# Attention backward: where the transposed output is scaled, and the order of matmuls around it

## The chip, the core and the metric

The kernel runs on one core of a Trainium2 chip. The core has five engines that run their own instruction queues, in order, and wait for each other through semaphores: TensorE (PE in the profile; its weight loads are PEld), VectorE (DVE), ScalarE (ACT), GpSimd (POOL) and SyncE (SP, which here issues DMAs). The metric is the device time of one execution in microseconds; lower is better.

## The reference

Forward and backward of two attention blocks on 2048 tokens, 16 heads of 28 channels: block A is linear attention, block B is softmax attention with one k and one v shared by all heads (MQA). The outputs are the forward result and the gradients of all eight inputs. The change lies in block B:

```python
def _B_ref(x, wq, wk, wv, wo):
    q = (x @ wq).reshape(B, S, H, Dh).transpose(0, 2, 1, 3)
    k = x @ wk
    v = x @ wv
    scores = jnp.einsum("bhqd,bkd->bhqk", q, k) * (Dh ** -0.5)
    p = _softmax(scores, axis=-1)
    o = jnp.einsum("bhqk,bkd->bhqd", p, v)
    return o.transpose(0, 2, 1, 3).reshape(B, S, H * Dh) @ wo
...
_out, _vjp = jax.vjp(_f, A_x, A_wqkv, A_wo, B_x, B_wq, B_wk, B_wv, B_wo)
_grads = _vjp(grad_out)
```

With e = exp(scores) unnormalised, l its row sums, and do the gradient that reaches o, the backward needs o/l, do/l, the row sum D of do times o/l, then dP = (do/l) v, dS = e (dP - D/l), and from these dQ, dK and dV.

## The kernel before

Block A and the projections of block B come first (up to about 205 us of the profile), then one long loop for the attention of block B, then the last projections. The change is in the loop alone. Its order of instructions is written by hand: the program text is the order of each engine's queue.

**Blocks and units.** A block b (64 of them) is 256 queries by two heads; eight units cover its 2048 keys, 256 keys to a unit (two tiles of 128). The loop runs over units u. At unit u it makes scores and exp of unit u, and, 16 units behind, dP and dS of unit w = u - 16. "Unit n" below is a unit with u mod 8 = n; `due(u, lag)` names the block whose first unit was `lag` units ago, so `due(u, 10)` holds in every unit 2.

**One unit, by engine.**
- TensorE: `rows_SD` issues eight matmuls of 32 rows by 128, 256 columns each. In its list `todo`, (0, h) is the scores of head h, (1, h) is dP of head h; each stands twice, for the two key tiles ("first half" and "second half"). The four kinds use four different groups of 32 rows of the array. Scores go to two of three PSUM banks `SB` in turn, dP to the two banks `DB`.
- ScalarE: exp of head 0 (L946), a copy of head 1's dP to SBUF (L960), exp of head 1 (L992).
- VectorE: dS of head 0 = dP times e, out of PSUM (L958), then a block transpose of the dS of unit u - 18 (L1039).
- GpSimd: dS of head 1 from ScalarE's copy (L961). It can't read PSUM.
- Even units: `o_dq` on TensorE, the "end product", accumulates o and dQ for two units in the bank `oq`. Odd units: `dk_m` accumulates dK (sixteen 32x32 matmuls of 512 columns).
- Every fourth unit SP issues a DMA transpose of eT to eN (L994), which dV reads: `dv_mm`, four matmuls a group, four groups a block, in even units behind `o_dq`.

**Once a block** o must be transposed, scaled and used. Unit 1: VectorE copies o from `oq` to `oTs` (L974). Unit 2: TensorE transposes it (`onat_T`, L809) into the `spare` bank, which is the bank of the scores just consumed and becomes the bank of head 0's scores of the next unit; then `o_norm`: VectorE takes 1/l from it (L818) and multiplies o by it into SBUF (L819); GpSimd makes the product do times o (L823), scales do (L826) and puts o over do in `do_nat` (L827, a cast). Unit 3: VectorE writes dQ of an older block (L977). Unit 4: `row_D`: VectorE sums the products along rows (L831), GpSimd multiplies by 1/l (L832). Unit 6: `don_T` transposes the scaled do (L840) into the spare bank, VectorE copies it out (L847). Unit 0, in most blocks: the output projection into the spare bank (`out_proj`), copied out by VectorE (L747). In half of the blocks GpSimd also copies queries twice (L851).

The order in one unit is: `rows_SD`; transposes and projections into the spare bank; exp, L958, L960, L961; `row_D`; L974, L977; `o_norm`; copies; exp of head 1 and the DMA transpose; `dk_m` or `o_dq` and `dv_mm`; L1039.

Of the kernel before, what the change touches and what calls it, by code (L numbers as in the profile page):

```python
# [9 lines left out]
ALU = mybir.AluOpType  # L10
AX = mybir.AxisListType
BF16 = mybir.dt.bfloat16
F32 = mybir.dt.float32
# [4 lines left out]
P = 128  # L18
# [7 lines left out]
def kernel(  # L26
# [21 lines left out]
    nc = tc.nc  # L48
# [39 lines left out]
    def flat(t):  # L88
        return t.rearrange("p a b -> p (a b)")
# [557 lines left out]
    NB = 64  # L647
    NU = NB * 8
    qT_B = [R1[:, g, :] for g in range(4)]
    vaug, kn, do_nat = vaug_, kn_, R2x[:, 0:NS, :]  # L650
    with ExitStack() as cs_:
# [7 lines left out]
        pw_ = cs_.enter_context(tc.tile_pool(name="cwk", bufs=4, side="right"))  # L659
# [5 lines left out]
        dsT, dsx, qX, don, doT, rl, prod = ({} for _ in range(7))  # L665
# [6 lines left out]
        def eN(b, c):  # L672
            return ENs[(2 * b + c // 2) % 6][:, 16 * (c % 2):16 * (c % 2) + 16, :]

        def mmt(out, lhsT, rhs, pos, start, stop):
            nc.tensor.matmul(out, lhsT=lhsT, rhs=rhs, start=start, stop=stop, tile_position=pos,  # L676
                             skip_group_check=True)

        def blk(b):
            qc, pair = divmod(b, 8)  # L680
            return qc, pair, pair // 2, pair % 2

        def rows_SD(u, sp, dp):
            b, tp = divmod(u, 8)
            w = u - 16
            qc, pair, g, hp = blk(b)
            todo = [(0, 0), (0, 1), (1, 0), (1, 1)] * 2
            if sp is not None and dp is not None and u % 2 == 0:
                todo = [(0, 0), (0, 1), (1, 0)] * 2 + [(1, 1)] * 2
            seen = {}  # L690
            for d in todo:
                if (dp if d[0] else sp) is None:
                    continue
                k, h = d
                t2 = seen.get(d, 0)
                seen[d] = 1
                t = 2 * tp + t2
                tc_ = slice(t * P, (t + 1) * P)
                oc = slice(t2 * 256, (t2 + 1) * 256)
                r = 64 * (1 - hp if k else hp) + 32 * h  # L700
                if k:
                    mmt(dp[h][:, oc], vT_rep[r:r + 32, tc_], doT[w // 8][r:r + 32, :], (r, 0), True, True)
                else:
                    mmt(sp[h][:, oc], kT_rep[r:r + 32, tc_], qT_B[g][r:r + 32, qc * 256:(qc + 1) * 256],
                        (r, 0), True, True)
# [8 lines left out]
        oTq = flat(R4).rearrange("p (t k) -> p t k", k=P)  # L714
# [85 lines left out]
        onps, tps2 = {}, {}  # L800

        def due(u, lag):
            b, r = divmod(u - lag, 8)
            return b if r == 0 and 0 <= b < NB else None

        def onat_T(b, bank):
            onp = bank[:, 0:P].rearrange("p (q h c) -> p q h c", q=2, h=2)
            for qb in range(2):
                nc.tensor.transpose(onp[:, qb, :, :].rearrange("p h c -> p (h c)"), oTs[0:64, qb * P:(qb + 1) * P],  # L809
                                    identF[0:64, 0:64], tile_position=(0, 0))  # L810
            onps[b] = onp

        def o_norm(b):
            onp = onps.pop(b)
            qc, pair, g, hp = blk(b)
            r_ = pw_.tile([P, 2, 2, 1], F32, name="rl")
            os_ = oTs[:, 0:P].rearrange("p (q h c) -> p q h c", q=2, h=2)
            nc.vector.reciprocal(out=r_[:], in_=onp[:, :, :, 0:1])  # L818
            nc.vector.tensor_tensor(out=os_, in0=onp[:, :, :, :], in1=r_[:].to_broadcast([P, 2, 2, 32]), op=ALU.mult)  # L819
            rl[b] = r_  # L820
            dnv = do_nat[:, 2 * qc:2 * qc + 2, pair * 64:pair * 64 + 64].rearrange("p q (h c) -> p q h c", c=32)
            prod[b] = pw_.tile([P, 2, 2, 32], F32, name="prod", bufs=1)
            nc.gpsimd.tensor_tensor(out=prod[b][:], in0=dnv, in1=os_, op=ALU.mult)  # L823
            dn = pw_.tile([P, 2, 2, 32], BF16, name="don", bufs=3)
            don[b] = dn
            nc.gpsimd.tensor_tensor(out=dn[:], in0=dnv, in1=r_[:].to_broadcast([P, 2, 2, 32]), op=ALU.mult)  # L826
            nc.gpsimd.tensor_copy(out=dnv, in_=os_)  # L827

        def row_D(b):
            Dq = pw_.tile([P, 2, 2, 1], F32, name="Dq")  # L830
            nc.vector.tensor_reduce(out=Dq[:, :, :, 0], in_=prod[b][:], axis=AX.X, op=ALU.add)  # L831
            nc.gpsimd.tensor_tensor(out=don[b][:, :, :, 0:1], in0=Dq[:], in1=rl[b][:], op=ALU.mult)  # L832

        def don_T(b, bank):
# [14 lines left out]
        def qc_copy(eng, st, qc, g, s):  # L849
            src = qT_B[g][:, qc * 256:(qc + 1) * 256].rearrange("p (b j s) -> p b j s", b=4, s=2)[:, :, :, s]  # L850
            eng.tensor_copy(out=st.rearrange("p (b s) a j -> p b s a j", s=2)[:, :, s, :, :],  # L851
                            in_=src.unsqueeze(2).to_broadcast([P, 4, 4, 32]))
# [36 lines left out]
        def o_dq(vs, ys):  # L889
            for v, y in zip(vs, ys):  # L890
                todo = [f(i) for f, i in ((o_mm, v), (dq_mm, y)) if 0 <= i < NU]
                for _ in range(2):
                    for g_ in todo:
                        next(g_)

        def dv_mm(dv_acc, b, h, qb):
            for c in range(4):
                rhs = eN(b, c).rearrange("p (u h t q) k -> p u h t q k", u=2, h=2,
                                                       t=2)[:, :, h, :, qb, :]
                mmt(dv_acc[32 * c:32 * c + 32, :], don[b][:, qb, h, :], rhs, (0, 32 * c),  # L900
                    b == 0 and h + qb == 0, b == NB - 1 and h + qb == 2)
# [15 lines left out]
        with tc.manual_schedule():  # L917
# [8 lines left out]
            for u in range(NU + 28):  # L926
# [3 lines left out]
                sp = [SB[(2 * u + h) % 3] for h in range(2)] if hasS else None  # L930
                dp = DB if hasD else None
                spare = SB[(2 * u + 2) % 3] if hasS else DB[u // 4 % 2] if u > 530 else SB[2]
                rows_SD(u, sp, dp)
                if (b := due(u, 10)) is not None:
                    onat_T(b, spare)
                if (b := due(u, 14)) is not None:
# [10 lines left out]
                if u == 1:  # L947
                    q_shift(pn3, shifts[3], [pd_.tile([P, 2, 512], BF16, name="dsT").rearrange("p a b -> p (a b)").bitcast(F32)
                                             for _ in range(1)])
                    dv_acc = psA.tile([P, 512], F32, name="aacc")  # L950
# [13 lines left out]
                if 0 <= gq < 4 and u < 448:  # L964
                    if gq == 0 and iq == 0:
                        qX[qq] = (pqb_ if qq % 2 else pqa_).tile([P, 4, 2, 512], BF16, name="qX")
                    if iq < 2:
                        qc_copy(nc.gpsimd, qst, qq, gq, iq)
                if (b := due(u, 12)) is not None:
                    row_D(b)  # L970
                if u == 7:
                    nc.vector.memset(oTs[64:128, :], 0.0)
                if (b := due(u, 9)) is not None:
# [1 line left out]
                if (b := due(u, 27)) is not None:  # L975
                    qc, pair, g, hp = blk(b)
                    nc.vector.tensor_scalar(out=qT_B[g][64 * hp:64 * hp + 64, qc * 256:(qc + 1) * 256],  # L977
                                            in0=oq[64:128, 0:256], scalar1=scale, scalar2=None, op0=ALU.mult)
                if (b := due(u, 10)) is not None:
                    o_norm(b)  # L980
                    if b in (15, 31, 47, 55, 63):
                        t0, t1 = 2 * (b // 8) - 2 * (b < 48), 2 * (b // 8) + 2
                        nc.sync.dma_start_transpose(oTq[:, 4 * (t0 % 4):4 * (t0 % 4) + 4 * (t1 - t0), :],
                                                    do_nat[:, t0:t1, :].rearrange("p q c -> p (q c)"))
                if (b := due(u, 14)) is not None:
                    don_copy(b)
                if op:
# [11 lines left out]
                if u % 2:  # L999
                    b, i = divmod(u - 27, 8)  # L1000
                    if 0 <= b < NB:
                        for m in range(2 * i, 2 * i + 4):
                            dk_m(b, m, (1 + (u == 519 and m == 2 * i + 1)) * (m % 2) if 519 <= u < 537 else 0)
                else:
                    o_dq((u - 2, u - 1), (u - 20, u - 19))
                    b, n = divmod(u - 20, 8)
                    for k in {0: (0, 1), 2: (2,), 6: (3,)}.get(n, ()) if 0 <= b < NB else ():
                        dv_mm(dv_acc, b, k // 2, k % 2)
                y = u - 18

                if 512 <= u < 528 and u % 2 == 0:
# [23 lines left out]
                if 0 <= y < NU:  # L1035
                    b, tp = divmod(y, 8)
                    if tp == 0:
                        dsx[b] = px_.tile([P, 8, 2, 2, 256], BF16, name="dsx")
                    nc.vector.transpose(  # L1039
                        out=dsx[b][:, tp, :, :, :].rearrange("p h t c -> p (h t c)").bitcast(F32),  # L1040
                        in_=dsT[y][:, :, :].rearrange("p h c -> p (h c)").bitcast(F32))

        dkvT, wqT, xb = post["dkvT"], post["wqT"], post["xb"]
        dkvn = post["dkvn"].rearrange("p (t c) -> p t c", c=64)
# [11 lines left out]
        for c in range(4):  # L1056
# [3 lines left out]
                                           in1=dk_sum[32 * c:32 * c + 32, :].rearrange("p (t i) -> p t i", i=32),  # L1060
# [91 lines left out]
```

## Time and profile before

| what | value |
|---|---|
| median of 3 runs | 1053.05 us (1052.27 to 1053.55) |
| profiled execution | 1052.68 us, its span 1050.9 us |
| busy: TensorE matmul, weight loads | 1008.4 us (96%), 486.6 us (46%) |
| busy: VectorE, ScalarE, GpSimd | 895.9 us (85%), 871.5 us (83%), 798.2 us (76%) |
| L961 GpSimd, 512 times | 1156 ns each |
| L1039, L958 VectorE, 512 times each | 699 ns, 668 ns each |
| L946, L960, L992 ScalarE, 512 times each | 612 ns, 617 ns, 629 ns each |
| L818, L819 VectorE, 64 times each | 159 ns, 292 ns each |
| L823, L826, L827, L832 GpSimd, 64 times each | 431, 399, 289, 216 ns each |
| L831, L847, L974, L977 VectorE, 64 times each | 276, 280, 405, 427 ns each |
| granted TensorE clock | full speed |

An engine starts its next instruction while the last results of the one before still drain: three ScalarE instructions of some 0.6 us in a unit of 1.5 us take less than their sum. So the mean duration of an instruction is not the time that it keeps the engine; for that the distance between two starts is read, where the second one waited for nothing. The loop's first exp (L946) starts at 207.7 us and the last at 977.0 us, 512 of them. Times of day in the prediction are microseconds from the start of the span.

### The profile page before, as it was taken

What the parts mean: (1) busy time and instruction counts of PE and PEld (TensorE: products, weight loads), DVE (VectorE), ACT (ScalarE), POOL (GpSimd) and SP (SyncE); (2) the same over time, 40 slices, a digit from 0 to 9 for tenths busy, and PEclk for the clock granted to TensorE, in tenths of its full rate; (3) what the DMA queues carried; (4) which work ended last, traced back from release to release, by engine and by line L of the source; (5) the groups of instructions that cost most, each with busy time, mean ns of one, the idle gap of its engine ahead of it and who ended that gap; (6) DMA issues with size and microseconds to landing.
All of it is one profiled execution on the core that took longest, in us unless ns stands there. A gap on an engine that the chain in (4) does not pass through costs nothing.

```text
span 1050.9 us, 40033 instructions
## 1 busy us (share of the span) xinstructions
PE 1008.4 (96%) x16236; PEld 486.6 (46%) x16245; DVE 895.9 (85%) x1781; ACT 871.5 (83%) x1743; POOL 798.2 (76%) x1044
## 2 busy tenths in 40 slices
PE   9999999998999999999999999999999999999998
PEld 5555554434444444444444444444444444444444
DVE  6897500669999999999999999999999999999942
ACT  6463122589999999999999999999999999999632
POOL 8601272238888998899899989988998999888860
PEclk9999999999999999999999999999999999999999
DMA  9879999299999999999999999999999999999973
GB/s 266 150 134 192 189 222 215 42 163 202 188 196 190 188 195 198 194 193 191 197 175 195 192 202 185 204 199 184 192 194 191 194 190 193 204 186 182 220 156 87
DMA packets 689058, 195.15 MB, mean 186 GB/s; under 512 B 670408, under 2 KB 686688, under 8 KB 688872
## 3 DMA queue, kind: packets, MB, share of 16 engines
q1 hardware_dynamic: 680392, 179.97, 102.1%
q0 software_dynamic: 4544, 9.46, 3.4%
q10 hardware_dynamic: 3936, 3.16, 1.0%
q8 instruction: 127, 2.08, 0.8%
q14 instruction: 59, 0.48, 0.1%
HBM read 12.60 MB, written 10.84 MB: 22 GB/s over the span
## 4 chain that ended last, share of the span: by engine, by line
PE 44%; ACT 33%; issue 14%; DVE 6%; POOL 2%; DMA 0%; ACTq 0%; DVEq 0%; POOLq 0%
ACT cp L960 17%; ACT eT L992 13%; PE agen L81 13%; PE aacc L676 10%; PE agen L676 10%; PE aacc L81 6%; ACT eT L946 2%; DVE dsT L958 2%; PE aacc L809 2%; DVE dsx L1039 2%; PE aacc L840 1%; POOL dsT L961 1%; DMA out_dram<-dsT 0%; PE agen L313 0%; PE agen L227 0%
## 5 line engine op out<-in xcount | busy, mean ns | idle before, releaser
L961 POOL TENSOR_TENSOR dsT<-cp,eT 128x512 bf16<-128x512 bf16 x512 | 587.7, 1156 | 78.9 <-ACT cp L960 73.2
L1039 DVE STREAM_TRANSPOSE dsx<-dsT 128x512 f32<-128x512 f32 x512 | 357.8, 699 | 2.8 <-POOL dsT L961 0.7
L676 PEld LDWEIGHTS <-R 32*128 32x128 bf16 (+1 forms) x9104 | 228.5, 94 | 275.0 <-issue 239.4
L958 DVE TENSOR_TENSOR dsT<-agen,eT 128x512 bf16<-128x512 f32 x512 | 341.9, 668 | 10.6 <-PE agen L676 5.4
L960 ACT ACTIVATE cp<-agen 128x512 bf16<-128x512 f32 x512 | 315.8, 617 | 11.5 <-PE agen L676 10.5
L946 ACT ACTIVATE eT<-aacc 128x512 bf16<-128x512 f32 x512 | 313.6, 612 | 13.6 <-PE aacc L676 4.3
L992 ACT ACTIVATE eT<-aacc 128x512 bf16<-128x512 f32 x512 | 322.2, 629 | 0.0
L676 PE MATMUL agen<-dsx,qX 32*32 32x512 bf16 x4024 | 264.0, 376 | 0.0
L676 PE MATMUL agen<-doT,R 32*128 32x256 bf16 x2048 | 246.7, 269 | 4.2 <-DVE dsT L958 2.5
L676 PE MATMUL aacc<-R,R 32*128 32x256 bf16 (+1 forms) x2240 | 218.5, 269 | 7.1 <-DVE oTs L819 2.0
L676 PE MATMUL agen<-eT,R 128*32 128x256 bf16 x2048 | 157.4, 274 | 0.1
L676 PE MATMUL agen<-dsT,R 128*32 128x256 bf16 x2048 | 156.6, 274 | 0.1
L676 PEld LDWEIGHTS <-qX 32*32 32x32 bf16 x4096 | 78.2, 89 | 111.7 <-issue 53.3
L676 PE MATMUL aacc<-eN,don 128*32 128x512 bf16 x1024 | 96.7, 379 | 0.0
L81 PEld LDWEIGHTS <-R 128*128 128x128 bf16 x517 | 40.9, 98 | 42.2 <-issue 12.0
L81 PE MATMUL agen<-R,R 128*128 128x448 bf16 (+1 forms) x174 | 41.1, 360 | 1.8 <-ACT R L229 0.8
L851 POOL COPY qst<-R 128x512 bf16<-128x512 bf16 x56 | 34.2, 611 | 2.9 <-DMA qX<-qst 2.8
L823 POOL TENSOR_TENSOR prod<-R,oTs 128x128 f32<-128x128 bf16 x64 | 27.6, 431 | 9.3 <-DVE oTs L819 9.3
L676 PEld LDWEIGHTS <-don 128*32 128x32 bf16 x1024 | 33.8, 97 | 0.5
L586 DVE TENSOR_TENSOR osb<-R 32x512 bf16<-32x512 bf16 x4 | 1.7, 413 | 34.7 <-ACT R L583 34.7
L262 POOL TENSOR_SCALAR wdq<-wdq 128x448 bf16<-128x448 bf16 x16 | 21.1, 1327 | 12.9 <-DVE phiT L243 12.9
L427 POOL COPY pk<-R 128x256 bf16<-128x256 bf16 x4 | 1.6, 399 | 37.7 <-DVE R L389 37.7
(234 smaller groups left out, 983.1 us busy)
## 6 DMA issues: line engine op xcount, KB each, us to landing
eN<-eT SPq DMA_TRANSPOSE x128
xa<-in_A_x_dram SPq DMA_DIRECT2D x8, 224.0 KB
ga<-in_grad_out_dram SPq DMA_DIRECT2D x4, 448.0 KB
out_dram<-osb ACTq DMA_DIRECT2D x16, 112.0 KB
xa<-in_grad_out_dram POOLq DMA_DIRECT2D x4, 448.0 KB, 9.4
out_dram<-wdq POOLq DMA_DIRECT2D x8, 224.0 KB, 5.8
eT<-in_grad_out_dram SPq DMA_DIRECT2D x4, 448.0 KB
eT<-in_B_x_dram SPq DMA_DIRECT2D x4, 448.0 KB
```

The lines of the kernel that those rows point to most:

```text
L81: nc.tensor.matmul(out_ap, lhsT=lhsT, rhs=rhs, start=start, stop=stop, tile_position=(0, 0))
L262: nc.gpsimd.tensor_scalar(out=wq_n[:, st, 0:D], in0=wq_n[:, st, 0:D], scalar1=1.0, scalar2=None, op0=ALU.min)
L676: nc.tensor.matmul(out, lhsT=lhsT, rhs=rhs, start=start, stop=stop, tile_position=pos, skip_group_check=True)
L809: nc.tensor.transpose(onp[:, qb, :, :].rearrange("p h c -> p (h c)"), oTs[0:64, qb * P:(qb + 1) * P], identF[0:64, 0:64], tile_position=(0 ...
L823: nc.gpsimd.tensor_tensor(out=prod[b][:], in0=dnv, in1=os_, op=ALU.mult)
L851: eng.tensor_copy(out=st.rearrange("p (b s) a j -> p b s a j", s=2)[:, :, s, :, :], in_=src.unsqueeze(2).to_broadcast([P, 4, 4, 32]))
L946: nc.scalar.activation(out=eT(u)[:, 0, :], in_=sp[0][:, :], func=ACT.Exp, scale=scale)
L958: nc.vector.tensor_tensor(out=dst[:, 0, :], in0=dp[0][:, :], in1=ew[:, 0, :], op=ALU.mult)
L960: nc.scalar.activation(out=cp[:, :], in_=dp[1][:, :], func=ACT.Copy)
L961: nc.gpsimd.tensor_tensor(out=dst[:, 1, :], in0=cp[:, :], in1=ew[:, 1, :], op=ALU.mult)
L992: nc.scalar.activation(out=eT(u)[:, 1, :], in_=sp[1][:, :], func=ACT.Exp, scale=scale)
L1039: nc.vector.transpose(out=dsx[b][:, tp, :, :, :].rearrange("p h t c -> p (h t c)").bitcast(F32), in_=dsT[y][:, :, :].rearrange("p h c -> p ...
```

## The change

- In odd units, and in all units at the ends of the loop, `todo` changes: odd units issue all four scores before the four dP; even units keep their list, now also where one of the two streams is absent.
- `o_norm` is split. `o_copy`, at its old place in unit 2, copies the transposed o unscaled out of PSUM to SBUF and has GpSimd make the product do times o. The new `o_norm` stands at the end of the unit, behind L1039: the reciprocal, now from SBUF; GpSimd scales do, and scales o where it cast it before. The DMA transposes of `do_nat` move with it.
- `row_D` moves from unit 4, ahead of L1039, to the end of unit 3, behind L1039. As the product now holds unscaled o, GpSimd multiplies the row sum by 1/l once more.
- `dv_mm` moves from behind `o_dq` to directly behind `rows_SD`, and its fourth group from unit 2 (of the next block) to unit 0.

```diff
-            todo = [(0, 0), (0, 1), (1, 0), (1, 1)] * 2
-            if sp is not None and dp is not None and u % 2 == 0:
+            todo = [(0, 0), (0, 1)] * 2 + [(1, 0), (1, 1)] * 2
+            if u % 2 == 0:
                 todo = [(0, 0), (0, 1), (1, 0)] * 2 + [(1, 1)] * 2
...
-        def o_norm(b):
+        def o_copy(b):
+            qc, pair, g, hp = blk(b)
             onp = onps.pop(b)
-            qc, pair, g, hp = blk(b)
-            r_ = pw_.tile([P, 2, 2, 1], F32, name="rl")
             os_ = oTs[:, 0:P].rearrange("p (q h c) -> p q h c", q=2, h=2)
-            nc.vector.reciprocal(out=r_[:], in_=onp[:, :, :, 0:1])
-            nc.vector.tensor_tensor(out=os_, in0=onp[:, :, :, :], in1=r_[:].to_broadcast([P, 2, 2, 32]), op=ALU.mult)
-            rl[b] = r_
+            nc.vector.tensor_copy(out=os_, in_=onp)
             dnv = do_nat[:, 2 * qc:2 * qc + 2, pair * 64:pair * 64 + 64].rearrange("p q (h c) -> p q h c", c=32)
+            onps[b] = os_, dnv
             prod[b] = pw_.tile([P, 2, 2, 32], F32, name="prod", bufs=1)
             nc.gpsimd.tensor_tensor(out=prod[b][:], in0=dnv, in1=os_, op=ALU.mult)
+
+        def o_norm(b):
+            os_, dnv = onps.pop(b)
+            r_ = pw_.tile([P, 2, 2, 1], F32, name="rl")
+            nc.vector.reciprocal(out=r_[:], in_=os_[:, :, :, 0:1])
+            rl[b] = r_
             dn = pw_.tile([P, 2, 2, 32], BF16, name="don", bufs=3)
             don[b] = dn
             nc.gpsimd.tensor_tensor(out=dn[:], in0=dnv, in1=r_[:].to_broadcast([P, 2, 2, 32]), op=ALU.mult)
-            nc.gpsimd.tensor_copy(out=dnv, in_=os_)
+            nc.gpsimd.tensor_tensor(out=dnv, in0=os_, in1=r_[:].to_broadcast([P, 2, 2, 32]), op=ALU.mult)
 
         def row_D(b):
             Dq = pw_.tile([P, 2, 2, 1], F32, name="Dq")
             nc.vector.tensor_reduce(out=Dq[:, :, :, 0], in_=prod[b][:], axis=AX.X, op=ALU.add)
+            nc.gpsimd.tensor_tensor(out=Dq[:], in0=Dq[:], in1=rl[b][:], op=ALU.mult)
             nc.gpsimd.tensor_tensor(out=don[b][:, :, :, 0:1], in0=Dq[:], in1=rl[b][:], op=ALU.mult)
...
                 rows_SD(u, sp, dp)
+                if u % 2 == 0:
+                    b, n = divmod(u - 20, 8)
+                    for k in {0: (0, 1), 2: (2,), 4: (3,)}.get(n, ()) if 0 <= b < NB else ():
+                        dv_mm(dv_acc, b, k // 2, k % 2)
...
-                if (b := due(u, 12)) is not None:
-                    row_D(b)
...
                 if (b := due(u, 10)) is not None:
-                    o_norm(b)
-                    if b in (15, 31, 47, 55, 63):
-                        t0, t1 = 2 * (b // 8) - 2 * (b < 48), 2 * (b // 8) + 2
-                        nc.sync.dma_start_transpose(oTq[:, 4 * (t0 % 4):4 * (t0 % 4) + 4 * (t1 - t0), :],
-                                                    do_nat[:, t0:t1, :].rearrange("p q c -> p (q c)"))
+                    o_copy(b)
...
                     o_dq((u - 2, u - 1), (u - 20, u - 19))
-                    b, n = divmod(u - 20, 8)
-                    for k in {0: (0, 1), 2: (2,), 6: (3,)}.get(n, ()) if 0 <= b < NB else ():
-                        dv_mm(dv_acc, b, k // 2, k % 2)
...
                         in_=dsT[y][:, :, :].rearrange("p h c -> p (h c)").bitcast(F32))
+                if (b := due(u, 10)) is not None:
+                    o_norm(b)
+                    if b in (15, 31, 47, 55, 63):
+                        t0, t1 = 2 * (b // 8) - 2 * (b < 48), 2 * (b // 8) + 2
+                        nc.sync.dma_start_transpose(oTq[:, 4 * (t0 % 4):4 * (t0 % 4) + 4 * (t1 - t0), :],
+                                                    do_nat[:, t0:t1, :].rearrange("p q c -> p (q c)"))
+                if (b := due(u, 11)) is not None:
+                    row_D(b)
```

## The prediction

> **Names.** A unit is one u of the main loop, a block is eight units, and unit n means u mod 8 = n. A unit has eight 256-column matmuls in `rows_SD`: scores for two heads, each in a first and a second half, and dP likewise. ScalarE takes exp of head 0's scores (L946), copies dP of head 1 (L960), takes exp of head 1's scores (L992). VectorE multiplies dP of head 0 (L958) and transposes (L1039). GpSimd multiplies dP of head 1 (L961).
>
> **What bounds the kernel.** First the busy time of each engine by stretch: the stretch where both streams of the loop run, then one block.
>
> ```profile
> core 0: us, PE busy (x) PEld busy (x) DVE busy (x) ACT busy (x) POOL busy (x), PEclk, DMA share, GB/s
> 250.00:977.00 727.00, 701.29 (x13784) 330.82 (x13783) 710.05 (x1381) 718.98 (x1445) 656.62 (x792) 1.00 1.17 192
> 579.66:591.75 12.09, 11.69 (x231) 5.63 (x231) 11.88 (x24) 12.02 (x26) 11.10 (x14) 1.00 1.19 188
> ```
>
> ScalarE is busy 99% of 727 us, VectorE 98%, GpSimd 90%, at full clock. But these are unions of overlapping instructions, so slack is read from distances between starts. ScalarE in that block:
>
> ```profile
> 580.63 0.66 ACT L992 ACTIVATE eT<-aacc 128x512 bf16<-128x512 f32 x1
> 581.17 0.61 ACT L946 ACTIVATE eT<-aacc 128x512 bf16<-128x512 f32 x1
> ...
> 583.09 0.65 ACT L960 ACTIVATE cp<-agen 128x512 bf16<-128x512 f32 x1
> 583.57 0.66 ACT L992 ACTIVATE eT<-aacc 128x512 bf16<-128x512 f32 x1
> 584.30 0.60 ACT L946 ACTIVATE eT<-aacc 128x512 bf16<-128x512 f32 x1
> ```
>
> Back to back, ScalarE starts one every 0.48 us (583.09 to 583.57). Into an odd unit it starts late: 0.54 into unit 1, 0.73 into unit 3. Read over all blocks between 423.21 and 880.63 us, a block takes 457.4 / 38 = 12.04 us, and L946 of the odd units is late by some 0.06, 0.26, 0.09 and 0.06 us (units 1, 3, 5, 7): 0.47 a block. That is what the change can win from ScalarE, no more.
>
> Unit 3 is late because of VectorE, seen in its timeline in the same block, and TensorE's:
>
> ```profile
> 582.78 0.64 DVE L958 TENSOR_TENSOR dsT<-agen,eT 128x512 bf16<-128x512 f32 x1
> 583.35 0.16 DVE L818 RECIPROCAL rl<-aacc 128x4 f32<-128x4 f32 x1
> 583.54 0.29 DVE L819 TENSOR_TENSOR oTs<-aacc,rl 128x128 f32<-128x128 f32 x1
> 583.75 0.70 DVE L1039 STREAM_TRANSPOSE dsx<-dsT 128x512 f32<-128x512 f32 x1
> 584.38 0.66 DVE L958 TENSOR_TENSOR dsT<-agen,eT 128x512 bf16<-128x512 f32 x1
> ...
> 586.14 0.69 DVE L958 TENSOR_TENSOR dsT<-agen,eT 128x512 bf16<-128x512 f32 x1
> 586.75 0.28 DVE L831 TENSOR_REDUCE Dq<-prod 128x4 f32<-128x128 f32 x1
> 586.94 0.70 DVE L1039 STREAM_TRANSPOSE dsx<-dsT 128x512 f32<-128x512 f32 x1
> ```
> ```profile
> 582.13 0.28 PE L676 MATMUL aacc<-R,R 32*128 32x256 bf16 x2
> ...
> 582.25 0.27 PE L676 MATMUL aacc<-R,R 32*128 32x256 bf16 x2
> ...
> 583.52 0.39 PE L676 MATMUL aacc<-eN,don 128*32 128x512 bf16 x4
> 583.89 0.28 PE L676 MATMUL aacc<-R,R 32*128 32x256 bf16 x2
> ```
>
> The transposed o lies in the bank of the next unit's first scores. It is free when L819 ends (583.84), and the scores start at 583.89, 0.05 later. dV (583.52) fills the time before it. The other odd units are late by order: the second half of the scores stands behind dP of head 1, which waits for L960 of the unit before (580.15 + 0.65 = 580.80; dP issues at 580.85, the scores' second half at 580.86).
>
> **The change, walked through this block.** Distances used: 0.48 between ScalarE's starts (0.49 after it waited); 0.12 from the first to the second half of scores, then 0.27 to its end and 0.03 to L946; 0.05 from the end of a VectorE or ScalarE instruction to the matmul that waits for it; 0.61 to 0.63 from L1039 to L958.
>
> *Scores first.* Unit 1: the second half can issue at 580.81 and end at 581.08; L946 then comes at ScalarE's own pace, 580.63 + 0.48 = 581.11, a gain of 0.06. dP still starts at 580.85, so dK behind it does not move. Where dP waits for nothing, as in unit 3, the odd unit's eight matmuls take longer: dP goes into other rows of the array and issues 0.12 behind the first scores, its second half 0.11 later, so dK starts 0.42 after the first scores, against 0.33 now (583.89 to 584.22).
>
> The Trainium skill says, in "TensorE: Matmul & The Clock Gate", section "The mechanism", that a weight load overlaps running matmuls only in another row group. This order puts two halves of the same rows behind each other, so that rule speaks against it. In this trace the second half at 582.25 starts 0.12 after a first half that runs 0.28, so the load did overlap; the sum goes by that row, and the rule's time is a rival below.
>
> *o copied.* No row shows a 128x128 f32 copy. L819 writes the same shape from the same bank in 292 ns on average, L974 copies 64x256 f32 in 405: I take 0.29 (lower end 0.27, the 112-column cast of L747; upper 0.40). It starts at 583.35 and ends at 583.64, so the scores of unit 3 start at 583.70 instead of 583.89. The four dV matmuls that stood there are gone to unit 0, so TensorE is ready (last product at 583.42 plus about 0.21). With 0.12 + 0.27 + 0.03, L946 comes at 584.11: a gain of 0.19. Without dV's removal it would be held to about 583.88.
>
> *Reciprocal and row sum moved behind L1039.* This gives part back. L1039 starts at 583.55 and ends its turn at 584.16; the reciprocal takes 0.19 (L818's turn today, now from SBUF; 0.12 to 0.30 as bounds), so L958 of unit 3 starts at 584.35 instead of 584.38. Then L977 585.04, L1039 585.39, the reduce 586.00 (its turn 0.19, 0.30 at worst), and L958 of unit 4 at 586.19: 0.05 later than now. Waiting behind it is dP of head 0 in unit 5, which needs L958's end: 586.94 instead of 586.89, and behind that dK and the next scores. GpSimd's product is ready for the reduce: it ends at about 585.3, 0.7 before; were that cover gone, L958 and dK would wait for the whole lack.
>
> *dV ahead.* Per block still sixteen matmuls in four groups, 0.22 a group. In unit 6 a group fills the 0.19 in which the don transposes wait for L992's bank today; in unit 0 one fills the same wait of the output projection (which starts at 579.90 instead of 579.87). In unit 4 two groups only change places with the end product. What they read is old: the transposed eT is issued 13 units (19 us) earlier and the DMA takes 4.8 to 5.9 us. Nothing waits there.
>
> *GpSimd.* The cast of 289 ns (L827) becomes a product (399 to 431 by L826 and L823), and one 128x4 product is added (216 by L832, up to 0.28 with the wait on itself): 0.33 to 0.42 a block. The block shown has the two query copies and 11.10 us busy, so 11.5 of some 11.9. Its dsT are read by L1039 two units later; the latest, now ready at 588.30, would be ready at 588.83, needed at 589.66. Hidden; without that 0.8 it would cost up to 0.4 a block. The five SP transposes of do_nat issue in the same place of SP's queue and wait some 0.1 longer for GpSimd; the next on SP waits for an exp of the next unit anyway. dP-only units at the end get two serial slots more, 0.11 in eight units: 0.4 taken, half of it.
>
> *Sum.* Following on: L946 of unit 5 at 586.98 (now 587.23), of unit 6 at 588.64 (588.67: the late dP has cost TensorE its lead), of unit 7 at 590.09 (590.20), of the next unit 0 at 591.54 (591.65); L958 there 591.64 (591.75). A second block from those times shifts everything by 0.11 again. The block at 604 us, which has no output projection, gives 0.14 by the same steps. With 0.115 a block and 62 blocks: 7.1 us. The profiled execution took 1052.68 (span 1050.9 and 1.8 around it); less 7.1, plus 0.4, is 1046.0, and the median of the runs is 0.37 above that execution: **1046** rounded. Its own range, from gains of 0.03 to 0.25 a block: 1038 to 1051.
>
> **Rivals.**
> - *The waits between engines go too.* VectorE's turns, each at its shortest, sum to about 11.72 a block with output projection; ScalarE's to 24 x 0.48 = 11.5. If only VectorE's turns are left, 0.31 x 62 = 19: 1033. For it: scores no longer wait for dP. Against: VectorE's turns themselves hardly shrink, and dP of unit 5 still hangs on L958.
> - *Nothing comes of it.* VectorE has as many instructions as before and was 98% busy; what leaves unit 2 returns in units 2 and 3: 1053.
> - *VectorE's small jobs hold dP (slower).* Reciprocal and reduce each stand directly before the L958 that frees dP's bank. The row L1039 to L958 is 0.73 into unit 4 today, not 0.62, for a reason that no wait shows. If both jobs carry 0.11 more, L958 of unit 4 comes at about 586.41 and dP of unit 5, dK and L946 of unit 6 are 0.2 later than in the walk, 0.17 later than now; that decides as soon as it exceeds the 0.11 won. A loss of 0.1 a block is 6, with the worst bounds 10: 1059.
> - *The scores' halves run one after another*: if the weights of the second half could load only after the first half has ended, it would start 0.37 (0.28, and 0.09 as the mean of one load) behind the first, L946 of units 1, 3, 7 late by 0.19, 0.07, 0.15, of unit 5 about equal; 0.3 a block after what is won: 1072. The rule of the Trainium skill named above would have it so; the 0.12 at 582.25 speaks against.
>
> **Chances.** Forecast 0.56; waits go too 0.17; nothing 0.12; VectorE's jobs 0.13; halves 0.02. A change of under 0.2% (2.1 us) can't be told from none. So faster 0.73, same 0.12, slower 0.15. The range 1033 to 1058 leaves out half of the second case and half of the slower ones, and holds the bounds of the copy and of the two small jobs.
>
> **What would show it.** The first scores of unit 3 follow the copy by 0.05 and L992-to-L946 there shrinks from 0.73 to about 0.6; in units 1 and 5 it is 0.48 to 0.50; L946 of even units, on pace today, shows some lateness in unit 6; L1039 to L958 into units 3 and 4 is 0.8 with the small job between. I am wrong if L958 of unit 4 is later by more than 0.1, if GpSimd's dsT end VectorE's idle time, or if dK of unit 3 starts more than 0.45 after its scores.

## The result, and the profile after

| | before | after |
|---|---|---|
| median | 1053.14 us (12 runs, 1051.86 to 1054.57) | 1050.93 us (12 runs, 1048.89 to 1052.52) |
| span of the profiled execution | 1050.9 us | 1049.1 us |
| first to last exp of the loop | 769.35 us | 767.93 us |

The ratio is 0.9977 with a 95% interval of 0.9967 to 0.9986: faster by 2.2 us, where 7 were forecast. In the new text exp of head 0 is L955, dS of head 0 L967, the copy of dP L969, dS of head 1 L970, exp of head 1 L995, the copy of o L817, the reciprocal L826, the reduce L835, the dQ write L984, the query copies L856 and their DMA transpose L860, eT's DMA transpose L997.

Busy time by engine over the loop, then ScalarE's timeline in the block from 579 us (start, duration, engine and line):

```profile
core 0: us, PE busy (x) PEld busy (x) DVE busy (x) ACT busy (x) POOL busy (x), PEclk, DMA share, GB/s
250.00:975.00 725.00, 697.21 (x13768) 322.28 (x13762) 705.28 (x1379) 716.17 (x1443) 669.94 (x850) 1.00 1.20 193
```
```profile
583.12 0.69 ACT L995 ACTIVATE eT<-aacc 128x512 bf16<-128x512 f32 x1
583.64 0.66 ACT L955 ACTIVATE eT<-aacc 128x512 bf16<-128x512 f32 x1
...
587.52 0.70 ACT L995 ACTIVATE eT<-aacc 128x512 bf16<-128x512 f32 x1
588.18 0.60 ACT L955 ACTIVATE eT<-aacc 128x512 bf16<-128x512 f32 x1
```

The busy shares hardly tell the two kernels apart, but the distances do. The exp of unit 3 now follows after 0.52 us instead of 0.73. That of unit 6 comes after 0.66: lateness moved three units on. Before, unit 6 kept pace, as here in the kernel before, one block later (0.48):

```profile
600.59 0.60 ACT L992 ACTIVATE eT<-aacc 128x512 bf16<-128x512 f32 x1
601.07 0.62 ACT L946 ACTIVATE eT<-aacc 128x512 bf16<-128x512 f32 x1
```

VectorE and TensorE of the changed kernel, in the stretch from 582 us, show the way it took:

```profile
582.92 0.26 DVE L817 COPY oTs<-aacc 128x128 f32<-128x128 f32 x1
...
583.73 0.12 DVE L826 RECIPROCAL rl<-oTs 128x4 f32<-128x4 f32 x1
583.79 0.65 DVE L967 TENSOR_TENSOR dsT<-agen,eT 128x512 bf16<-128x512 f32 x1
584.47 0.43 DVE L984 TENSOR_SCALAR R<-agen 64x256 bf16<-64x256 f32 x1
...
585.44 0.24 DVE L835 TENSOR_REDUCE Dq<-prod 128x4 f32<-128x128 f32 x1
585.71 0.69 DVE L967 TENSOR_TENSOR dsT<-agen,eT 128x512 bf16<-128x512 f32 x1
```
```profile
583.24 0.28 PE L676 MATMUL aacc<-R,R 32*128 32x256 bf16 x2
...
583.34 0.28 PE L676 MATMUL aacc<-R,R 32*128 32x256 bf16 x2
...
586.13 0.39 PE L676 MATMUL aacc<-R,R 32*128 32x256 bf16 x4
586.46 0.39 PE L676 MATMUL agen<-doT,R 32*128 32x256 bf16 x4
586.78 1.04 PE L676 MATMUL agen<-dsx,qX 32*32 32x512 bf16 x16
587.76 0.28 PE L676 MATMUL aacc<-R,R 32*128 32x256 bf16 x2
```

The copy ends at 583.18 and unit 3's scores start at 583.24. In unit 4 L967 starts 0.27 after the reduce and ends at 586.40; dP of unit 5, whose scores were done issuing by 586.25, starts at 586.46, then dK, and only then the scores of unit 6 (587.76).

So the block is shorter, though by less than forecast. Block lengths are read from the exp of head 0 in every eighth unit. In blocks 16 to 55 plain blocks alternated between 12.03 and 11.97 us before, and take 11.91 or 11.92 now, 0.085 less. In blocks 4 to 14 it is 0.04 less (11.96 now), and in the last seven full ones, from 56 on, 0.02 (12.21 now). Plain blocks alone would so give some 4 us. The rest is lost in four long blocks: blocks 5 and 6 took 13.4 and 13.6 us (13.2 and 12.0 before), blocks 38 and 39 took 12.9 and 12.5 (12.0 and 12.3). All four have query copies or follow a block that has them. The page of the changed kernel names a wait at the query copies (line, count, busy and mean, then idle time before it and its cause), which stood on the page of before with 2.8 us:

```profile
L856 POOL COPY qst<-R 128x512 bf16<-128x512 bf16 x56 | 34.4, 614 | 6.6 <-DMA qX<-qst 5.9
```

One such stall, on SP's, GpSimd's and VectorE's timelines of the changed kernel (idle time and its cause in brackets):

```profile
264.17 11.11 SPq L997 DMA_TRANSPOSE eN<-eT  x2
275.33 1.31 SPq L860 DMA_TRANSPOSE qX<-qst  x1
276.74 10.57 SPq L997 DMA_TRANSPOSE eN<-eT  x2
287.42 2.12 SPq L860 DMA_TRANSPOSE qX<-qst  x1
```
```profile
280.53 0.61 POOL L856 COPY qst<-R 128x512 bf16<-128x512 bf16 x1 [1.94 <-DMA qX<-qst]
```
```profile
282.29 0.71 DVE L1039 STREAM_TRANSPOSE dsx<-dsT 128x512 f32<-128x512 f32 x1 [1.07 <-POOL dsT L970]
```

SP has no gap in which it waits. Two transposes of eT and one of the queries keep it for 12.1 to 12.6 us a block (275.33 to 287.42, and 264.17 to 276.74), more than the block itself takes, so in the four of eight blocks with query copies it can't keep up. In the first such blocks it carries a backlog besides: the exp of unit 27, before any of these copies, ends at 247.35, and its transpose starts at 251.71. The copy at 280.53 may not overwrite the one query buffer before the transpose issued at 275.33 has read it. GpSimd stands for 1.94 us, and VectorE's block transpose waits 1.07 for GpSimd's dS. SP was as full in the kernel before, 12.3 us from one query transpose to the next:

```profile
274.19 1.30 SPq L855 DMA_TRANSPOSE qX<-qst  x1
...
286.45 1.25 SPq L855 DMA_TRANSPOSE qX<-qst  x1
```

### The profile page after: what moved, and what is told of

Read it like the earlier page. It is cut to its first block, busy times and chain, and to the rows that moved or that the text cites. A ratio compares the mean times of both kernels' runs of the same rounds, so it can differ in the third digit from the quotient of the medians.

```text
span 1049.1 us, 40115 instructions
## 1 busy us (share of the span) xinstructions
PE 1006.1 (96%) x16245; PEld 477.9 (46%) x16245; DVE 891.7 (85%) x1781; ACT 870.0 (83%) x1743; POOL 813.8 (78%) x1108
## 3 DMA queue, kind: packets, MB, share of 16 engines
q8 instruction: 127, 2.08, 0.8%
## 4 chain that ended last, share of the span: by engine, by line
PE 61%; DVE 13%; ACT 10%; issue 8%; POOL 7%; DMA 1%; DVEq 0%; POOLq 0%; ACTq 0%
PE agen L676 24%; PE aacc L676 15%; PE agen L81 13%; DVE dsT L967 6%; PE aacc L81 6%; POOL dsT L970 5%; ACT cp L969 4%; ACT eT L995 3%; ACT eT L955 2%; DVE dsx L1039 2%; DVE doT L852 2%; PE aacc L809 2%; DVE Dq L835 1%; DVE R L984 1%; POOL prod L821 1%
## 5 line engine op out<-in xcount | busy, mean ns | idle before, releaser
L970 POOL TENSOR_TENSOR dsT<-cp,eT 128x512 bf16<-128x512 bf16 x512 | 585.6, 1158 | 52.9 <-ACT cp L969 48.4
L1039 DVE STREAM_TRANSPOSE dsx<-dsT 128x512 f32<-128x512 f32 x512 | 357.1, 698 | 5.1 <-POOL dsT L970 3.0
L676 PEld LDWEIGHTS <-R 32*128 32x128 bf16 (+1 forms) x9104 | 239.3, 94 | 258.9 <-issue 209.6
L967 DVE TENSOR_TENSOR dsT<-agen,eT 128x512 bf16<-128x512 f32 x512 | 342.8, 670 | 12.3 <-PE agen L676 5.2
L969 ACT ACTIVATE cp<-agen 128x512 bf16<-128x512 f32 x512 | 324.3, 633 | 13.1 <-PE agen L676 12.7
L955 ACT ACTIVATE eT<-aacc 128x512 bf16<-128x512 f32 x512 | 324.5, 634 | 12.6 <-PE agen L676 4.3
L995 ACT ACTIVATE eT<-aacc 128x512 bf16<-128x512 f32 x512 | 329.7, 644 | 0.0
L676 PE MATMUL agen<-doT,R 32*128 32x256 bf16 x2048 | 242.5, 270 | 7.6 <-DVE dsT L967 4.9
L676 PE MATMUL aacc<-R,R 32*128 32x256 bf16 (+1 forms) x2240 | 208.2, 267 | 19.7 <-DVE doT L852 8.9
L676 PE MATMUL agen<-eT,R 128*32 128x256 bf16 x2048 | 155.3, 273 | 0.1
L676 PE MATMUL aacc<-eN,don 128*32 128x512 bf16 x1024 | 90.5, 387 | 0.0
L856 POOL COPY qst<-R 128x512 bf16<-128x512 bf16 x56 | 34.4, 614 | 6.6 <-DMA qX<-qst 5.9
L676 PEld LDWEIGHTS <-don 128*32 128x32 bf16 x1024 | 20.8, 93 | 40.6 <-issue 40.6
```

The source lines that it names most:

```text
L955: nc.scalar.activation(out=eT(u)[:, 0, :], in_=sp[0][:, :], func=ACT.Exp, scale=scale)
L967: nc.vector.tensor_tensor(out=dst[:, 0, :], in0=dp[0][:, :], in1=ew[:, 0, :], op=ALU.mult)
L969: nc.scalar.activation(out=cp[:, :], in_=dp[1][:, :], func=ACT.Copy)
L970: nc.gpsimd.tensor_tensor(out=dst[:, 1, :], in0=cp[:, :], in1=ew[:, 1, :], op=ALU.mult)
L995: nc.scalar.activation(out=eT(u)[:, 1, :], in_=sp[1][:, :], func=ACT.Exp, scale=scale)
L1039: nc.vector.transpose(out=dsx[b][:, tp, :, :, :].rearrange("p h t c -> p (h t c)").bitcast(F32), in_=dsT[y][:, :, :].rearrange("p h c -> p ...
```

## The experiments

Three theories were on trial. **V**: the reduce ahead of L967 in unit 4 makes dP and dK of unit 5 and the scores of unit 6 late. **O**: scores ahead of dP cost TensorE what the rest wins. **G**: GpSimd stalls on the query buffer's DMA, and more so in a faster loop. Each run's ratio compares it with the kernel before on the same chip; that kernel's medians were 1053.1 to 1054.2 us on the chips used, so a difference between the medians of two runs is uncertain by about as much. Waits and block lengths are from one execution of each.

**The reduce back in unit 4.**
```diff
+                if (b := due(u, 12)) is not None:
+                    row_D(b)
                 if u == 7:
...
-                if (b := due(u, 11)) is not None:
-                    row_D(b)
```


> The changed kernel with the row sum back in unit 4, between L958 and the transpose. Theory V (the reduce ahead of L958 of unit 4 makes dP of unit 5, dK and the scores of unit 6 late; that is where the gain of unit 3 went): L958 of unit 4 0.17 to 0.27 us earlier after the transpose of unit 3, lateness of unit 6's first exp falls from 0.27 to under 0.1 us a block, blocks of about 11.85 instead of 11.91 us, 1046 to 1048 us. Theory O (the score-first rows cost TensorE what the rest wins): nothing changes in unit 6, 1050 to 1052. Theory G (stalls of GpSimd behind the query DMA): regular blocks stay 11.91, but the row sum no longer holds VectorE in a stalled block, 1049 to 1050.

1049.71 us (ratio 0.9962, 0.9948 to 0.9976). Plain blocks are 11.83 to 11.85 us, as V has it. In VectorE's timeline the product of unit 4 follows the transpose by 0.73 us instead of 0.89, and the exp of unit 6 is nearer to pace: from unit 5's to unit 6's it is 1.54 us on average over units 144 to 448, against 1.71 in the changed kernel (about 1.45 is on pace):

```profile
584.46 0.70 DVE L1041 STREAM_TRANSPOSE dsx<-dsT 128x512 f32<-128x512 f32 x1
585.19 0.69 DVE L967 TENSOR_TENSOR dsT<-agen,eT 128x512 bf16<-128x512 f32 x1
```

But the median, above V's range, has only 1.2 of the more than 4 us that 62 blocks would give: GpSimd waits 6.0 us on the query DMA in seven places, and blocks of 12.5 to 13.8 us take the rest. V is right for the plain block, but this move alone brings back little of the time.

**The query transpose ahead of eT's on SP.**
```diff
+                    if 0 <= gq < 4 and iq == 1 and u < 448:
+                        qc_T(qst, qq, gq)
                     if u % 4 == 3:
                         nc.sync.dma_start_transpose(ENs[u // 4 % 6][:, :, :],
                                                     ETs[u // 4 % 5][:, :, :, :].rearrange("p a b c -> p (a b c)"))
-                    if 0 <= gq < 4 and iq == 1 and u < 448:
-                        qc_T(qst, qq, gq)
```


> The changed kernel with the DMA transpose of the query copies issued ahead of the transpose of eT in the same unit, so that the one query buffer is free earlier. Theory G: GpSimd's idle time on the query DMA (5.9 us in four waits) goes to about 0, blocks of over 12.4 us in the middle of the loop disappear, 1048 us. Theories V and O: the stalls are a matter of this one profile, the median stays 1050 to 1052.

1046.61 us (0.9932, 0.9918 to 0.9947), 4.3 less than the changed kernel. The plain blocks are the same 11.92; no wait on the query DMA is left in the trace, and most long blocks between 260 and 700 us are gone. SP issues each query transpose one transpose of eT earlier:

```profile
255.66 1.26 SPq L860 DMA_TRANSPOSE qX<-qst  x1
...
267.92 1.31 SPq L860 DMA_TRANSPOSE qX<-qst  x1
...
280.80 1.23 SPq L860 DMA_TRANSPOSE qX<-qst  x1
```

SP is as full as before (12.3 and 12.9 us from one to the next); what waits now is eT's transpose, whose reader comes more than ten units later. G stands.

**The same in the kernel before.** The edit is the same.

> The kernel before with the query transpose ahead of eT's alone. If the stalls on the query DMA belong to the kernel as such: 4 us won as in the changed kernel, 1049. If they are in the main a product of the change (theory G as the reason for the missing gain): the kernel before wins at most its own two waits, 2.8 us of GpSimd's idle time, 1051 to 1053.

1051.07 us (0.9975, 0.9966 to 0.9985): 2.2 us less than the kernel before on that chip (1053.30), half of what the changed kernel wins. Without the stalls on both sides the change is worth 1051.07 - 1046.61 = 4.5 us instead of 2.2; from first to last exp the two profiles take 768.06 and 763.98 us. So the stalls were in the kernel, and with the change they cost about twice as much. They also differ from one execution to the next: without them nine executions lie within 0.8 us and five within 1.0, while the twelve of the changed kernel spread over 3.6.

**The old order in odd units.**
```diff
-            todo = [(0, 0), (0, 1)] * 2 + [(1, 0), (1, 1)] * 2
-            if u % 2 == 0:
+            todo = [(0, 0), (0, 1), (1, 0), (1, 1)] * 2
+            if sp is not None and dp is not None and u % 2 == 0:
```


> The changed kernel with the old order in odd units (scores and dP in turn). Theory O: dK of units 3 and 7 up to 0.1 us earlier, unit 6 less late, 1047 to 1049. Theory V: unit 6 stays late by 0.2 or more and the odd units get their 0.06 lateness back, 1051 to 1053.

1052.51 us (0.9987, 0.9979 to 0.9996): the time is as V said, but not the place. The exp of unit 5 is late now (1.74 us behind unit 4's, against 1.46), because the second half of its scores again stands behind dP, which waits for L967 of unit 4; unit 6 is on pace (1.45). The score-first order lets unit 5 pass and hands the lateness to unit 6, at a small profit. O falls.

**dV back behind the end product.**

> The changed kernel with dV behind the end product again and its fourth group in unit 2. Theory V: unit 6 stays late; in unit 2 dV holds the scores of unit 3 to about 0.36 us behind its issue, 0.1 to 0.2 us later than now, 1051 to 1056. If dV ahead costs more than it hides (theory O in a wider sense): 1048 to 1050.

1056.47 us (1.0028, 1.0019 to 1.0038), slower than the kernel before and a little more than V's range. Its edit moves the `dv_mm` loop back behind `o_dq`, with its groups in units 4, 6 and 2 as before the change. Blocks are 12.08; the exp of unit 3 is 1.72 us behind unit 2's, as before the change (1.70), and that of unit 6 is late as well (1.68). The copy of o is worth nothing while dV stands ahead of unit 3's scores.

**One part alone, on the kernel before.**

> The kernel before with the new order of the odd units' matmuls alone. Theory V: odd units 1 and 5 lose their lateness of 0.06 and 0.09 us, unit 3 keeps 0.26 as the o bank holds it; VectorE's chain is not shortened, 1050 to 1053. Theory O: dK later by up to 0.1 us in units 3 and 7, 1053 to 1057.

> The kernel before with dV moved alone. The bank of unit 3 is then free at the end of the old scaling (583.84 in the walk) and TensorE is ready before, so unit 3 wins 0.05 at most: 1050 to 1053. If dV ahead of the transposes costs: 1054 to 1057.

> The changed kernel with both the old matmul order and the old dV place: of the change only the copy of o, the scaling on GpSimd and the moved reciprocal and row sum are left. Theory V: dV in unit 2 still holds the scores of unit 3, so the copy wins nothing there, while the reduce still makes unit 6 (or, with the old order, unit 5) late: blocks of 12.1 to 12.2 us, 1056 to 1060. If the copy alone brought the gain: 1048 to 1051.

| part alone | median, us | ratio, 95% interval | plain blocks, us | GpSimd's wait on the query DMA |
|---|---|---|---|---|
| order of odd units | 1053.69 | 1.0001 (0.9992 to 1.0010) | 11.93, 11.96 | 9.6 us, 8 times |
| dV ahead | 1054.12 | 1.0003 (0.9993 to 1.0013) | 12.02, 11.97 | 3.7 us, 4 times |
| o copied, scaled later | 1058.04 | 1.0033 (1.0022 to 1.0044) | 12.17, 12.05 | 4.4 us, 4 times |

The order alone shortens the plain block by 0.055 us and the median shows nothing of it. That median lies in O's range, but a shorter plain block is not what O says, and the run has the longest waits on the query DMA. The waits don't simply follow the length of a block, though: the o part has the longest blocks and still 4.4 us of them. So the part of G that a faster loop makes the stalls dearer is shown for the whole change alone.

The dV move alone can't be told from no change. The o part alone is slower, as V said: with dV in its old place unit 3 stays late (1.67 us), and unit 5 becomes late (1.71) behind the reduce. The parts together are faster although none is faster alone.

**Both remedies, and one product less.** First the reduce in unit 4 and the query transpose first; then, on top, 1/l squared right after o is scaled, so that one GpSimd product stands behind the reduce instead of two:
```diff
+            rl2[b] = pw_.tile([P, 2, 2, 1], F32, name="rl2")
+            nc.gpsimd.tensor_tensor(out=rl2[b][:], in0=r_[:], in1=r_[:], op=ALU.mult)
...
-            nc.gpsimd.tensor_tensor(out=Dq[:], in0=Dq[:], in1=rl[b][:], op=ALU.mult)
-            nc.gpsimd.tensor_tensor(out=don[b][:, :, :, 0:1], in0=Dq[:], in1=rl[b][:], op=ALU.mult)
+            nc.gpsimd.tensor_tensor(out=don[b][:, :, :, 0:1], in0=Dq[:], in1=rl2[b][:], op=ALU.mult)
```


> The changed kernel with the row sum back in unit 4 and the query transpose ahead of eT's. Theories V and G together: regular blocks 11.84 us as with the row sum moved alone, no GpSimd wait on the query DMA, 1042 to 1043 us, the best so far. If the late don of the run with the row sum moved alone (23 us of waits of its transposes) is a cost of its own and not a consequence of the stalls: 1045 to 1047.

> The run with the row sum in unit 4 and the query transpose first, with the two 128x4 products behind the row sum made one: 1/l is squared on GpSimd right after o is scaled, so that only one product lies between the reduce and the don transposes. If the late don is what is left (18.6 us of its transposes' waits, 56 times, in the run without this): the wait falls by 0.28 us a time, the blocks of 12.27 us come down toward 11.85, 1042 to 1044. If that wait is hidden: 1045 to 1046 again.

1045.31 us (0.9921, 0.9908 to 0.9935): plain blocks of 11.84 without the stalls, but above the 1042 to 1043 that V and G together gave. The transposes of the scaled do (`don`) wait for GpSimd, above all in blocks with query copies and an output store on GpSimd (12.27 us):

```profile
PEld L845 <- POOL don L837: 18.6, 56, 0.8
```

With the squared 1/l: 1043.62 us (0.9895, 0.9879 to 0.9910), that wait down to 8.3 us in 34 places, plain blocks mostly 11.76 to 11.80. This beats both kernels: it is 1.05% below the kernel before, and the changed kernel 0.23%. What stands out are three blocks of 12.5 to 13.5 us from 773 us on, and there SP's queue is at work again. With the query transposes first and a faster loop, those of eT come later: they start up to 11.6 us behind their exp, and TensorE's dV waits for them in four places, in these blocks and one more (total, count, longest):

```profile
PE aacc L676 <- DMA eN<-eT: 2.3, 4, 1.2
```

GpSimd, too, waits for the query DMA again, 1.7 us in four places. No run took these waits away.

**Why L967 of unit 4 waits for the reduce's end.** No wait shows there, and in the kernel before the same product came 0.73 us after the transpose and not 0.62. The Trainium skill ("VectorE: DVE Perf Modes", section "Two Vector instructions with no wait between them") says that an instruction starts only when all earlier ones are done if its input begins in another quadrant of 32 partitions than the last read of the same memory. The dQ write L984 reads PSUM from partition 64, L967 of unit 4 is the next to read PSUM, from 0. The edit puts the dQ write ahead of unit 3's L967 and takes it out of its old place:
```diff
+                if (b := due(u, 27)) is not None:
+                    qc, pair, g, hp = blk(b)
+                    nc.vector.tensor_scalar(out=qT_B[g][64 * hp:64 * hp + 64, qc * 256:(qc + 1) * 256],
+                                            in0=oq[64:128, 0:256], scalar1=scale, scalar2=None, op0=ALU.mult)
                 if hasD:
                     dst = pd_.tile([P, 2, 512], BF16, name="dsT")
```


> The changed kernel with VectorE's dQ write (L984, it reads PSUM from partition 64) moved ahead of the dS product in unit 3. The dS product of unit 4 starts only after the reduce has ended (0.27 us from start to start, no overlap) although no wait shows. If the reason is that it is the first to read PSUM from partition 0 after the dQ write, which read from partition 64: the gap moves to the dS product of unit 3, and the reduce's turn ahead of unit 4's falls to 0.19 or 0.20. If it is something of unit 4 itself: 0.27 there as now. The time is not what this run is for; the dQ write delays dP's bank in unit 3 by some 0.4 us, so 1050 to 1058.

1053.57 us (0.9998, 0.9988 to 1.0007). In VectorE's timeline (the product is L971 and the dQ write L965 in this text) the product of unit 3 now waits for the whole dQ write, 0.46 us from start to start, and that of unit 4 follows the reduce by 0.17 where it took 0.27:

```profile
584.08 0.43 DVE L965 TENSOR_SCALAR R<-agen 64x256 bf16<-64x256 f32 x1
584.54 0.69 DVE L971 TENSOR_TENSOR dsT<-agen,eT 128x512 bf16<-128x512 f32 x1
...
585.77 0.24 DVE L835 TENSOR_REDUCE Dq<-prod 128x4 f32<-128x128 f32 x1
585.94 0.68 DVE L971 TENSOR_TENSOR dsT<-agen,eT 128x512 bf16<-128x512 f32 x1
```

Over the blocks between units 144 and 448 the two distances are 0.46 and 0.17 us on average. The rule explains this gap. Blocks of the changed kernel bear it out without an edit. The copy of don (L852) reads PSUM from partition 64 in every second block and from 0 in the others; between units 144 and 448 it starts 0.72 us behind the product in front of it in the former and 0.61 in the latter, and the next product starts 0.74 and 0.63 behind its transpose. The copy of o (L981) also reads 64 partitions, but from 0, and holds nothing: the transpose starts 0.33 behind it, before its 0.41 us are over. So it is the start that counts, not the number of partitions.

## Why the prediction was right or wrong

- *What bounds the kernel*: right for a plain block. ScalarE is near its pace, held by VectorE through the banks; the lateness in unit 3 was the o bank. SP's queue, which bounds the blocks with query copies, is missing.
- *Scores first*: right in mechanism. The second half follows the first by 0.10 (583.24 to 583.34), dK of unit 3 starts 0.43 after its scores (0.42 was worked out). The rival that halves run one after another did not happen.
- *The copy*: 0.27 us on average (0.29 taken), and unit 3's exp follows after 0.52 us, where about 0.6 was expected. That dV had to leave unit 2 for it is shown by the runs with dV back.
- *Small jobs behind L1039*: the reciprocal's turn is 0.06 where 0.19 was taken, but the reduce's is 0.27 where 0.19 was taken, for the reason just shown. The two errors nearly cancel: L967 of unit 4 starts 2.07 us after unit 3's exp (583.64 to 585.71), and the walk had 2.08 (584.11 to 586.19). Unit 6 is late as it was there.
- *The sum*: 0.115 us a block, 62 times, is the first step that failed. It is a term that was mis-sized. This is how long the exps of head 0 come after that of the unit before, in us, as the mean of the medians of even and odd blocks from 18 to 55 (the other units change by less than 0.01):

  | exp of unit | 1 | 3 | 5 | 6 | 7 |
  |---|---|---|---|---|---|
  | before | 1.49 | 1.68 | 1.54 | 1.45 | 1.50 |
  | after | 1.46 | 1.48 | 1.46 | 1.69 | 1.49 |
  | change | -0.03 | -0.20 | -0.08 | +0.24 | -0.02 |
  | change in the walk | -0.06 | -0.13 | -0.06 | +0.22 | -0.08 |

  Units 3 and 5 won more than was worked out, units 1 and 7 less, and unit 6 lost a little more: 0.085 a block. And these blocks do not stand for the others. In blocks 4 to 14 and in the last seven, where VectorE makes other copies in unit 0, unit 1 comes 0.02 and 0.04 later instead of earlier, and the blocks win 0.04 and 0.02. Over the loop that is some 4 us instead of 7.1, as the two profiles without stalls on the query DMA show (768.06 - 763.98 = 4.1, with one other long block in each).
- *GpSimd*: "Hidden" is the second step that failed. It compared busy time with the length of a block and the lateness of dS with its reader, and took the query copies as busy time only. They also wait, for a DMA that stands on SP behind eT's. SP was asked only about the order of five transposes of do_nat; its own time in the blocks with queries (12.3 us against 12.0) was not added up, though the page showed the wait. By the medians the stalls cost 2.2 us before and 4.3 after, so they took about 2 us of the gain. One of the prediction's signs of being wrong came with them: GpSimd's dS ends VectorE's idle time, 3.0 us in seven waits, against 0.7 in two before.
- *The end of the program*: put at 0.4 us more; from the last exp of head 0 to the end of the span it took 73.9 us before and 73.4 after, 0.5 less.
- *Rivals*: the range held the time. "VectorE's small jobs" had the right place, unit 6, but its price, 0.11 more for both jobs, did not come: the reduce took 0.08 more and the reciprocal 0.13 less.

Together: 4.1 from the loop and 0.5 from the end, less about 2 for the dearer stalls, is close to the 2.2 us measured. The forecast's 1046 was met by the changed kernel with the query transpose moved (1046.61), but that is not the change that was forecast, and partly chance: its plain block is still the smaller gain, and it also lacks the stalls that the kernel before had.

What stays open: why unit 1 gets later in the first and the last blocks, which no run separated; why the stalls are dearer in some executions than in others; and why a transpose of eT keeps SP for 5.4 us.

## What to carry to other kernels

When a loop is about to get faster, add up the time of every queue per round, the DMA-issuing one too; one that is already as long as the round will take the gain back at whoever waits for it, and changing the order in that queue can hand the wait to another reader. A gain worked out for one round should be checked on rounds of each kind before it is multiplied. A scaling moved out of a shared bank helps only as far as nothing else stands ahead of the bank's next user, so parts that look separate are worth testing together. A short instruction placed ahead of a long one that frees a bank delays the other engine by its turn, and that turn can be several times longer in one place than in another.

## What the runs showed of the hardware

The price of a small VectorE instruction depends on what the next one reads: the same reduce took 0.19 us of VectorE's time ahead of a transpose, 0.17 ahead of a product that could overlap it, and 0.27 ahead of one whose PSUM input began at another partition than the last PSUM read. And a reciprocal of 128x4 from SBUF took only 0.06 us from its start to the next instruction, which did not need its result, and 0.16 where the dQ write, which reads PSUM from partition 64, stood behind it; out of PSUM, ahead of the product that needed it, it was 0.19.

A DMA transpose keeps the engine that issues it: eT's kept SP for 4.8 to 6.0 us (median 5.4) in the changed kernel, a query buffer's for 1.2 to 2.1 (median 1.3).
